# Linear attention into a Swish feed-forward: sharing three pieces of batch 1's preparation differently between engines

## The chip, the cores and the metric

The kernel runs on one core of a Trainium2 chip. A core has a matrix engine (TensorE, "PE" in the profile), a vector engine (VectorE, "DVE"), a scalar engine (ScalarE, "ACT"), a general engine (GpSimd, "POOL") and a sync engine (SyncE, "SP") that here only issues transfers. Each engine runs its own instructions in order and waits on semaphores for others. The metric is device time in microseconds, the median of several executions.

## The reference, cut to what matters

```python
def phi(x):                     # elu(x) + 1
    return np.where(x > 0, x, np.exp(x) - 1.0) + 1.0
q_p, k_p = phi(q), phi(k)                       # 8 batches, 8 heads, 576 rows, 64 columns
kv  = einsum('bhsd,bhse->bhde', k_p, v)
z   = sum(k_p, axis=2)
num = einsum('bhsd,bhde->bhse', q_p, kv)
den = einsum('bhsd,bhd->bhs', q_p, z)[..., None] + 1e-06
x   = (num / den) -> transposed to (4608 rows, 512)
h   = x @ w_in                                  # 512 x 2048
g   = h * (1.0 / (1.0 + np.exp(-beta * h)))     # beta: one number for each of 2048 columns
out = g @ w_out                                 # 2048 x 512
```

## The kernel before, in words

The work goes batch by batch. For each batch the rows are first prepared: phi of q and k (an exp on ScalarE, a max-and-add `r` and a minimum on VectorE), v copied beside a column of ones into `vaug`, the product of k and v (`kv_both`, tile `kvp`), q transposed, the numerators and denominators (`numers`, tile `nps`), their quotient `xs`, and the transpose of that, `xT`. Then come the two matrix products: `h_phase` makes 16 steps of 4 matmuls of 512 columns, each followed by ScalarE's silu into `g`; `y_phase` makes 4 tiles `y_ps` of 16 matmuls each, which are copied to `y_sb` and stored. Each row count is 576 = 4 x 128 + 64; the last 64 rows of all batches are gathered and treated as a ninth round.

The silu is computed with the scale beta, and w_out is divided by beta once: `w_out_scale(i)` multiplies the i-th of four quarters, chunk by chunk (c from 0 to 3), by `rbeta` into bfloat16. The float weights are loaded into space that is free early on (`g`'s second buffer and `stage`).

The order of instructions is written out by hand (`manual_schedule`); the framework adds the semaphore waits that data and buffers need. Batch 0 and 1 are special. While TensorE works on batch 0's y, the other engines prepare batch 1: `phi_all(1, ...)`, `v_copy(..., 1, pr)` for two pairs of heads pr, `q_trans(1, ...)` (transposes on TensorE, four copies to `qT` on ScalarE), `kv_both(1)`, `numers_1`, `numers_1_last`, and `x_trans(1, t, ...)` (transposes on TensorE, a copy to `xT`). Between them, by hand, stand the pieces of batch 0's y: `y_mm(b, t, i, ...)` adds four matmuls (quarter i of w_out) to y tile t. Two more things are put there: the scaling of w_out's last quarter, `w_out_scale(3, (1, 3))`, whose chunks 1 and 3 ScalarE makes and 0 and 2 VectorE, and the exps of batch 2 (`phi_part(2, ...)`), which must come before the first silu of batch 1, as exp and silu need different tables in ScalarE.

PSUM, the memory that TensorE writes to, has eight banks. Four are the ring `mm` (tiles `y_ps`, `h_ps`, one `tp`); a tile gets the slot that was given back longest ago, and waits until its last reader has finished. The other four hold small tiles for batch 0's start and, from batch 1's kv on, two pair tiles of two banks (`num_tile`: `kvp`, `nps`, `tp`, `qop`). In `h_phase` of batch 1, steps 3 and 4 take pair tiles in place of ring tiles. The transposes `qop` (after step 6) and the kv product of batch 2 (after step 8) take pair tiles too.

The loads of q, k, v for the first batches and of the weights are issued from GpSimd's queue at the start; its copies stand in the same queue. Stores and transposing transfers are issued from SP's.

Of the kernel before, what the change touches and what calls it, by code (L numbers as in the profile page):

```python
# [10 lines left out]
ALU = mybir.AluOpType  # L11
# [5 lines left out]
def kernel(  # L17
# [10 lines left out]
    nc = tc.nc  # L28

    B, H, S, D = q.shape  # L30
# [6 lines left out]
    J = S // G  # L37
# [17 lines left out]
    vaug = [consts.tile([P, 2, J, 2, 66], BF16, name=f"vaug{i}") for i in range(2)]  # L55
    w_in_sb = [consts.tile([P, KC, 512], BF16, name=f"w_in{i}") for i in range(4)]
    w_out_sb = [consts.tile([P, 4, DM], BF16, name=f"w_out{i}") for i in range(4)]
# [7 lines left out]
    w_out_f = [  # L65
        a.rearrange("p (c m) -> p c m", c=4)
        for a in (g_f[:, 0:2048], g_f[:, 2048:4096], stage[:, 0:2048], stage[:, 2048:4096])
    ]
# [71 lines left out]
    def phi_part(b, a, pr, x, j0=0, j1=J):  # L140

        if j0 == 0:
            st[b, a, pr, "e"] = work.tile([P, 2, J, D], BF16, tag="e", name="e", bufs=4)
        nc.scalar.activation(st[b, a, pr, "e"][:, :, j0:j1], x[:, :, j0:j1], ACTF.Exp)  # L144
# [17 lines left out]
    def places(b, pr):  # L162

        return slice(2 * pr, 2 * pr + 2) if b == 0 else slice(pr, 4, 2)

    def xin(b, a, pr):
        if b == 0 and a == "q":
            return q0f[:, places(b, pr)]
        return (xk if a == "k" else xq)[b % NX][:, places(b, pr)]

    def v_copy(eng, b, pr):
        src = vb[b % 2] if b < 3 else vf[b % 2]
        eng.tensor_copy(  # L173
            vaug[b % 2][:, pr, :, :, 0:D], src[:, places(b, pr)].rearrange("p h j d -> p j h d")
        )

    def k_quads(b, pr, dst, mov):
# [49 lines left out]
    def num_tile(name):  # L227
        return numps.tile([P, 2, 512], F32, tag="num", name=name)
# [4 lines left out]
    def kv_both(b):  # L233

        t = num_tile("kvp")
        for pr in range(2):
            kv_pair(b, pr, [t[:, hh, pr * EA : (pr + 1) * EA] for hh in range(2)])
        if b == 1:
            nc.vector.tensor_copy(kv1[:, 0], t[:, 0, 0 : 2 * EA])
            nc.scalar.copy(kv1[:, 1], t[:, 1, 0 : 2 * EA])  # L240
            return
        st[b, "kvd"] = work.tile([P, 2, 2 * EA], BF16, tag="kv_bd", name="kvd")
        nc.vector.tensor_copy(st[b, "kvd"], t[:, :, 0 : 2 * EA])

    def copy(eng, dst, src):
        if eng is nc.scalar:
            nc.scalar.copy(dst, src)  # L247
        else:
            eng.tensor_copy(dst, src)  # L249
# [219 lines left out]
    def h_mm(b, x, ff, hp, c0=0, c1=512):  # L469
        for kc in range(KC):  # L470
            nc.tensor.matmul(  # L471
                hp[:, c0:c1],
                w_in_sb[ff // 4][:, kc, (ff % 4) * P : (ff % 4 + 1) * P],
                x[:, kc, c0:c1],
                start=(kc == 0), stop=(kc == KC - 1), skip_group_check=True,
            )

    def silu(b, ff, hp):
        nc.scalar.activation(  # L479
            g_sb[b % 2][:, ff, :], hp, ACTF.Silu, scale=beta_c[:, ff : ff + 1]  # L480
        )

    def mm_tile(name):
        return mmps.tile([P, 512], F32, tag="mm", name=name)

    def y_mm(b, t, i, yp, c0=0, c1=512):
        for c in range(4):
            ff = 4 * i + c
            nc.tensor.matmul(  # L489
                yp[:, c0:c1],  # L490
                g_sb[b % 2][:, ff, t * P : (t + 1) * P],
                w_out_sb[i][:, c, c0:c1],
                start=(ff == 0), stop=(ff == FC - 1), skip_group_check=True,
            )

    def rows(b, j):
        return out[b * S : (b + 1) * S, :].rearrange("(g j) m -> j g m", j=J)[j]

    def y_out(b, t, yp, c0=0, c1=512, queues=(nc.sync, nc.sync), copier=nc.vector):
        y_sb = work.tile([P, DM], F32, tag="y_sb", name="y_sb", bufs=3)  # L500
        copy(copier, y_sb[:, c0:c1], yp[:, c0:c1])
        for i in range(2):
            dst = rows(b, 2 * t + i) if b < B else rows(2 * t + i, J - 1)
            queues[i].dma_start(out=dst[:, c0:c1], in_=y_sb[i * G : (i + 1) * G, c0:c1])
# [28 lines left out]
    def v_copies(b):  # L533
        for pr in range(2):
            v_copy(nc.gpsimd, b, pr)
# [4 lines left out]
    rbeta = consts.tile([P, FC], F32)  # L540
# [183 lines left out]
        if ff == 5:  # L724
            q_odd_trans(0, misc_bf()[:, 0:256])

    def w_out_scale(i, acts=()):
        for c in range(4):
            ff = 4 * i + c
            if c in acts:  # L730
                nc.scalar.mul(w_out_sb[i][:, c, :], w_out_f[i][:, c, :], rbeta[:, ff : ff + 1])
            else:
                nc.vector.tensor_scalar(
                    w_out_sb[i][:, c, :], w_out_f[i][:, c, :], rbeta[:, ff : ff + 1],
                    None, ALU.mult,
                )

    load(nc.gpsimd, xq[2], q, 2)
    load(nc.gpsimd, xk[2], k, 2)
# [2 lines left out]
    for i in range(3):  # L742
        w_out_scale(i)
    yps = [mm_tile("y_ps") for _ in range(4)]
    phi_all(1, "q")
    phi_all(1, "k")
    for i in range(2):
        for t in range(4):
            y_mm(0, t, i, yps[t])
    v_copy(nc.gpsimd, 1, 1)  # L750
    v_copy(nc.vector, 1, 0)
    y_mm(0, 0, 2, yps[0])
    y_mm(0, 1, 2, yps[1])
    q_trans(1, (0, 1), num0_tile().bitcast(BF16), (nc.scalar, nc.scalar))
    y_mm(0, 2, 2, yps[2])
# [1 line left out]
    num0_pool.__exit__(None, None, None)  # L757
    misc_pool.__exit__(None, None, None)
    numps = ctx.enter_context(tc.tile_pool(name="numps", bufs=2, space=bass.MemoryType.PSUM))
    y_mm(0, 3, 2, yps[3], 0, 256)  # L760
    kv_both(1)
    y_mm(0, 3, 2, yps[3], 256, 512)
    w_out_scale(3, (1, 3))
    numers_1()
    phi_tile(2, "q")
# [9 lines left out]
    copies = [x_trans(1, t, nc.scalar, tp[:, t - 1]) for t in (1, 2)]  # L775
    for f in copies:
        f()
    y_out(0, 1, yps[1])
    y_mm(0, 3, 3, yps[3], 0, 256)
    x_trans(1, 3, nc.vector, num_tile("tp")[:, 0].bitcast(BF16))()  # L780
    y_mm(0, 3, 3, yps[3], 256, 512)
    for pr in range(2):
        phi_part(2, "k", pr, xin(2, "k", pr))
    phi_part(2, "q", 1, xin(2, "q", 1))
    y_out(0, 2, yps[2])
    for pr in range(2):
        phi_relu(2, "k", pr, xin(2, "k", pr))
    y_out(0, 3, yps[3])
# [6 lines left out]
    def run(side, n):  # L795
        for f in side.get(n, ()):
            f()

    def h_phase(b, x, side):
        for ff in range(FC):  # L800

            if b == 1 and ff in (3, 4):
                hp = num_tile("h_ps2")[:, 0]
            else:
                hp = mm_tile("h_ps")
            h_mm(b, x, ff, hp)
            silu(b, ff, hp)
            run(side, ff)
# [25 lines left out]
    for b in range(1, B + 1):  # L834
# [22 lines left out]
        if m < B:  # L857
# [7 lines left out]
            if m + 1 < B:  # L865
                at(sy, 10, lambda: phi_exps(m + 1, "k"))
        h_phase(b, xT[b % 3] if b < B else xT_tail, sh)
        y_phase(b, sy, last=(b == B))

# [29 lines left out]
```

## Time and profile before

| | us |
|---|---|
| median of 12 runs | 286.94 |
| lowest, highest | 286.22, 289.76 |
| the profiled execution's own time | 289.11 |
| its span | 287.3 |
| PE busy | 278.0 |
| ACT busy | 162.0 |
| DVE busy | 106.2 |
| POOL busy | 38.0 |

The span runs from the first to the last instruction in the trace; the execution's own time has another 1.8 us around it. In the lines that follow, a chain or timeline line begins with the start in the span and the duration, both in us; L12 is line 12 of the kernel; "out<-in" are tiles; "x8" counts instructions; a bracket gives the idle time of the engine just before, and what ended it. The mean granted clock of TensorE is 0.988 of full speed.

### The profile page before, as it was taken

The numbers are of one execution on the slowest core, as the hardware profiler recorded it, in microseconds if no ns is written. First come the engines' busy times: TensorE is split into PE (matmuls) and PEld (weight loads), VectorE is DVE, ScalarE is ACT, GpSimd is POOL, SyncE is SP. The second block draws the span as 40 slices with busy tenths as digits, with TensorE's granted clock in tenths as the row PEclk, the third lists the DMA queues.
The fourth block names the chain that finished last, engine by engine and source line by source line (L and its number), as shares of the span: only waits on it lengthen the run. The fifth ranks groups of instructions, "written<-read, shape, count | busy, mean of one in ns | idle before, by whom it ended". The sixth has DMA issues, their size and how long they took to land.

```text
span 287.3 us, 5995 instructions
## 1 busy us (share of the span) xinstructions
PE 278.0 (97%) x2504; PEld 140.0 (49%) x2504; DVE 106.2 (37%) x261; ACT 162.0 (56%) x221; POOL 38.0 (13%) x50
## 2 busy tenths in 40 slices
PE   7799998999999999999999999999999999999994
PEld 2585445544664544454445444544444444444443
DVE  5742656912952283128311931191015100110012
ACT  5659866985766861786188707840860076017500
POOL 8622120306002200310040001200000000000000
PEclk9879999999999999999999999999999999999999
DMA  7999999579969946983898349445403410230032
GB/s 217 201 214 390 227 281 194 133 116 265 185 129 264 202 78 147 273 150 78 149 270 147 80 119 263 100 80 137 96 2 79 114 39 0 49 81 19 0 73 74
DMA packets 51723, 41.03 MB, mean 143 GB/s; under 512 B 31584, under 2 KB 43120, under 8 KB 51696
## 3 DMA queue, kind: packets, MB, share of 16 engines
q1 hardware_dynamic: 38800, 23.61, 34.6%
q0 software_dynamic: 12736, 16.91, 30.0%
q8 instruction: 19, 0.31, 0.5%
q10 hardware_dynamic: 160, 0.13, 0.2%
q14 instruction: 8, 0.07, 0.1%
HBM read 36.71 MB, written 9.44 MB: 161 GB/s over the span
## 4 chain that ended last, share of the span: by engine, by line
PE 90%; ACT 5%; DMA 3%; issue 1%; DVE 0%; POOL 0%; DVEq 0%; POOLq 0%
PE y_ps L489 43%; PE h_ps L471 40%; DMA xk<-in_k_dram 3%; ACT e L144 2%; PE h_ps L668 1%; PE nps L315 1%; ACT g L479 1%; PE nps L184 1%; PE kvp L184 1%; ACT xT L247 1%; PE nps L634 1%; PE warm_ps L133 1%; PE nps_m L315 0%; ACT L479 0%; ACT qT L247 0%
## 5 line engine op out<-in xcount | busy, mean ns | idle before, releaser
L479 ACT ACTIVATE g<-h_ps,beta_c 128x512 bf16<-128x512 f32 x144 | 97.7, 689 | 89.0 <-PE h_ps L471 88.5
L489 PE MATMUL y_ps<-w_out,g 128*128 128x512 bf16 (+3 forms) x632 | 127.4, 360 | 0.0
L471 PE MATMUL h_ps<-xT,w_in 128*128 128x512 bf16 x496 | 109.0, 379 | 0.4 <-ACT xT L247 0.3
L489 PEld LDWEIGHTS <-g 128*128 128x128 bf16 x632 | 60.7, 98 | 61.6 <-issue 0.2
L471 PEld LDWEIGHTS <-w_in 128*128 128x128 bf16 x560 | 54.6, 98 | 65.2 <-DVE xT L249 0.4
L249 DVE COPY y_sb<-y_ps 128x512 f32<-128x512 f32 (+2 forms) x36 | 24.2, 672 | 80.3 <-PE y_ps L489 80.3
L421 DVE TENSOR_SCALAR den<-nps 128x12 f32<-128x12 f32 x14 | 2.3, 165 | 63.2 <-PE nps L315 63.2
L144 ACT ACTIVATE e<-xk 128x1152 bf16<-128x1152 bf16 x16 | 17.8, 1156 | 3.6 <-DMA xk<-in_k_dram 2.5
L83 POOL DMA_DIRECT2D xq<-in_q_dram x7 | 5.2, 746 | 93.4 <-DVE phi_k L155 42.7
L144 ACT ACTIVATE e<-xq 128x1152 bf16<-128x1152 bf16 x14 | 15.6, 1156 | 0.1
L412 DVE TENSOR_TENSOR xs<-nps,rden 128x512 bf16<-128x512 f32 (+1 forms) x29 | 15.0, 557 | 0.5
L471 PE MATMUL h_ps<-xT_tail,w_in 128*128 128x512 bf16 x64 | 14.0, 379 | 0.0
L173 POOL CAST vaug<-vf 128x1152 bf16<-128x1152 f32 x10 | 11.2, 1148 | 18.2 <-DMA vf<-in_v_dram 13.9
L155 DVE TENSOR_TENSOR phi_q<-e,r 128x1152 bf16<-128x1152 bf16 (+2 forms) x17 | 11.7, 717 | 2.7 <-ACT e L144 2.4
L155 DVE TENSOR_TENSOR phi_k<-e,r 128x1152 bf16<-128x1152 bf16 x16 | 11.5, 751 | 0.3 <-ACT e L144 0.2
L133 PE MATMUL warm_ps<-xT 128*128 128x512 bf16 x23 | 8.2, 501 | 1.5 <-DVE xT L96 1.5
L144 ACT ACT_TABLE_LOAD x6 | 7.7, 1283 | 2.8 <-DMA xq<-in_q_dram 2.6
L479 ACT ACT_TABLE_LOAD x6 | 7.7, 1283 | 0.1
L148 DVE TENSOR_SCALAR r<-xk 128x1152 bf16<-128x1152 bf16 x16 | 7.6, 509 | 0.4 <-DMA xk<-in_k_dram 0.4
L184 PEld LDWEIGHTS <-phi_k 64*64 64x64 bf16 x576 | 5.9, 108 | 3.6 <-issue 3.6
L83 POOL DMA_DIRECT2D xk<-in_k_dram x9 | 6.8, 755 | 4.7 <-DMA g<-in_moe_w_out_dram 2.0
L173 POOL COPY vaug<-vf 128x1152 bf16<-128x1152 bf16 x3 | 4.0, 1345 | 19.0 <-DMA vf<-in_v_dram 19.0
(96 smaller groups left out, 118.9 us busy)
## 6 DMA issues: line engine op xcount, KB each, us to landing
out_dram<-y_sb SPq DMA_DIRECT2D x70, 128.0 KB, 2.4
vf<-in_v_dram SPq DMA_DIRECT2D x5, 1152.0 KB, 6.6
xq<-in_q_dram POOLq DMA_DIRECT2D x7, 576.0 KB, 9.8
xk<-in_k_dram POOLq DMA_DIRECT2D x7, 576.0 KB, 11.9
w_in<-in_moe_w_in_dram POOLq DMA_DIRECT2D x4, 512.0 KB, 12.9
g<-in_moe_w_out_dram POOLq DMA_DIRECT2D x2, 1024.0 KB, 18.1
stage<-in_moe_w_out_dram POOLq DMA_DIRECT2D x2, 1024.0 KB, 20.6
stage<-in_q_dram SPq DMA_DIRECT2D x2, 576.0 KB, 4.1
```

Source lines behind the costliest of these rows:

```text
L83: return eng.dma_start(out=dst[:, h0 : h0 + n].rearrange("p h j d -> p h (j d)"), in_=rows.rearrange("(i p) e -> p i e", p=P)[:, h0 : h0 + n],
L133: nc.tensor.matmul(warm_ps[:, 0:cols], warm[:, 0:P], warm[:, 0:cols], start=True, stop=True)
L144: nc.scalar.activation(st[b, a, pr, "e"][:, :, j0:j1], x[:, :, j0:j1], ACTF.Exp)
L148: nc.vector.tensor_scalar(r, x, 0.0, 1.0, ALU.max, ALU.add)
L155: nc.vector.tensor_tensor(st[b, a][:, pr, j0:j1].rearrange("p j (h d) -> p j h d", h=2), st[b, a, pr, "e"][:, :, j0:j1].rearrange("p h j d ...
L173: eng.tensor_copy(vaug[b % 2][:, pr, :, :, 0:D], src[:, places(b, pr)].rearrange("p h j d -> p j h d"))
L184: nc.tensor.matmul(dst[hh][c], st[b, "k"][r, pr, j, c], mov(r, j, h), start=(j == 0), stop=(j == J - 1), skip_group_check=True,)
L249: eng.tensor_copy(dst, src)
L412: nc.vector.tensor_mul(out, num, rd[..., None].to_broadcast(list(num.shape)))
L471: nc.tensor.matmul(hp[:, c0:c1], w_in_sb[ff // 4][:, kc, (ff % 4) * P : (ff % 4 + 1) * P], x[:, kc, c0:c1], start=(kc == 0), stop=(kc == K ...
L479: nc.scalar.activation(g_sb[b % 2][:, ff, :], hp, ACTF.Silu, scale=beta_c[:, ff : ff + 1])
L489: nc.tensor.matmul(yp[:, c0:c1], g_sb[b % 2][:, ff, t * P : (t + 1) * P], w_out_sb[i][:, c, c0:c1], start=(ff == 0), stop=(ff == FC - 1), ...
```

## The change

`v_copy` gets a range of the nine groups of rows, and the copy for batch 1's second pair of heads is divided: GpSimd copies groups 0 to 3, ScalarE groups 4 to 8. VectorE copies the first pair as before. In `w_out_scale(3, (1, 3))` chunks 1 and 3 are made by GpSimd instead of ScalarE, and every `y_mm` goes through its four chunks in the order 0, 2, 1, 3. The y piece (tile 3, quarter 2), which stood half before and half after `kv_both(1)`, stands before it whole. The output copy of y tile 1 moves behind the copy of x's fourth tile and behind the exps of batch 2 in the order of the program. In batch 1's `h_phase`, steps 0 and 1 take the pair tiles, where 3 and 4 did.

```diff
-    def v_copy(eng, b, pr):
+    def v_copy(eng, b, pr, j0=0, j1=J):
         src = vb[b % 2] if b < 3 else vf[b % 2]
-        eng.tensor_copy(
-            vaug[b % 2][:, pr, :, :, 0:D], src[:, places(b, pr)].rearrange("p h j d -> p j h d")
+        copy(
+            eng,
+            vaug[b % 2][:, pr, j0:j1, :, 0:D],
+            src[:, places(b, pr), j0:j1].rearrange("p h j d -> p j h d"),
         )
...
     def y_mm(b, t, i, yp, c0=0, c1=512):
-        for c in range(4):
+        for c in (0, 2, 1, 3):
...
-    def w_out_scale(i, acts=()):
+    def w_out_scale(i, pool=()):
         for c in range(4):
             ff = 4 * i + c
-            if c in acts:
-                nc.scalar.mul(w_out_sb[i][:, c, :], w_out_f[i][:, c, :], rbeta[:, ff : ff + 1])
-            else:
-                nc.vector.tensor_scalar(
-                    w_out_sb[i][:, c, :], w_out_f[i][:, c, :], rbeta[:, ff : ff + 1],
-                    None, ALU.mult,
-                )
+            (nc.gpsimd if c in pool else nc.vector).tensor_scalar(
+                w_out_sb[i][:, c, :], w_out_f[i][:, c, :], rbeta[:, ff : ff + 1],
+                None, ALU.mult,
+            )
...
-    v_copy(nc.gpsimd, 1, 1)
+    v_copy(nc.gpsimd, 1, 1, 0, 4)
+    v_copy(nc.scalar, 1, 1, 4, J)
     v_copy(nc.vector, 1, 0)
...
-    y_mm(0, 3, 2, yps[3], 0, 256)
+    y_mm(0, 3, 2, yps[3])
     kv_both(1)
-    y_mm(0, 3, 2, yps[3], 256, 512)
     w_out_scale(3, (1, 3))
...
-    y_out(0, 1, yps[1])
     y_mm(0, 3, 3, yps[3], 0, 256)
     x_trans(1, 3, nc.vector, num_tile("tp")[:, 0].bitcast(BF16))()
     y_mm(0, 3, 3, yps[3], 256, 512)
     for pr in range(2):
         phi_part(2, "k", pr, xin(2, "k", pr))
     phi_part(2, "q", 1, xin(2, "q", 1))
-    y_out(0, 2, yps[2])
+    for t in (1, 2):
+        y_out(0, t, yps[t])
...
-            if b == 1 and ff in (3, 4):
+            if b == 1 and ff < 2:
                 hp = num_tile("h_ps2")[:, 0]
             else:
                 hp = mm_tile("h_ps")
```

## The prediction

> **What bounds the kernel now.** I read the page first: the engines' totals and the chain that ended last.
>
> ```profile
> PE 278.0 (97%) x2504; PEld 140.0 (49%) x2504; DVE 106.2 (37%) x261; ACT 162.0 (56%) x221; POOL 38.0 (13%) x50
> PE 90%; ACT 5%; DMA 3%; issue 1%; DVE 0%; POOL 0%; DVEq 0%; POOLq 0%
> ```
>
> TensorE is the bound, and from 61 us to the end the chain in order of time is TensorE alone. Only what moves TensorE's instructions before that counts. All edits act between 39 and 61 us, so I read the chain there:
>
> ```profile
> 43.11 0.46 PE nps L269 x8
> 43.57 0.02 issue
> 43.59 1.08 ACT qT L247 x2
> 44.67 0.04 issue
> 44.72 0.84 PE kvp L184 x71
> ...
> 45.65 0.30 DVE kv L239
> ...
> 45.98 0.28 ACT kv L240
> ...
> 46.30 0.54 PE nps L315 x44
> 46.84 1.93 PE y_ps L489 x8
> ...
> 49.38 0.58 ACT xT L247
> 49.97 1.06 ACT e L144
> 51.03 0.96 ACT xT L247 x2
> 51.99 3.17 ACT e L144 x3
> 55.16 0.02 issue
> 55.18 1.28 ACT L479
> 56.46 0.01 issue
> 56.47 2.43 ACT g L479 x4
> ```
>
> Two stretches are not TensorE's: batch 1's kv product waits for ScalarE's last qT copy, and from 49.38 to 58.90 ScalarE is full without a gap (exps, x copies, table load, silus). The timeline by engine gives the cover of the moved work and the second stall:
>
> ```profile
> 42.28 1.07 ACT L247 COPY qT<-nps 128x512 bf16<-128x512 bf16 x2 [2.44 <-PE nps L269]
> 39.88 1.76 POOL L173 COPY vaug<-vf 128x1152 bf16<-128x1152 bf16 x1 [9.78 <-DMA vf<-in_v_dram]
> 50.88 2.23 POOL L173 COPY vaug<-vf 128x1152 bf16<-128x1152 bf16 x2 [9.25 <-DMA vf<-in_v_dram]
> 58.94 0.27 PE L288 MATMUL qop<-identity,phi_q 128*128 128x128 bf16 x2 [0.70 <-ACT g L479]
> ```
>
> ScalarE is idle 2.44 us before the qT copies, GpSimd 9.25 us after its v copy, and the qop transposes wait for ScalarE's fourth silu, whose PSUM tile they take.
>
> **What the Trainium skill says.** (1) GPSIMD Engine Reference, "Elementwise — side-by-side cycle accounting": about 1.03 cycles an element for small bodies, 1.8 for an ordinary good loop. The trace agrees for casts: 1148 ns for 1152 float elements. (2) SBUF — State Buffer, "Who interferes with whom": GpSimd and certain VectorE operations lock each other out of a shared port. The trace agrees: GpSimd's v copy took 1756 ns beside VectorE's work at 39.88, and 1137 ns alone. (3) ScalarE: Activation LUTs, "What ACT_TABLE_LOAD costs": 0.833 ns an element; copies lie in every table set by its section on table sets. The trace agrees: no table load stands between exps and copies.
>
> **The change part by part.** Times are those of the profiled execution.
>
> *v in three.* v of batch 1 lands at 39.82 (landing records). GpSimd keeps 4 of 9 groups, 512 elements: 1.14 x 512/1152 = 0.5 us alone, at most about 1.2 with the lockout of 0.62 seen now. ScalarE gets 640: its 512-element copy takes 585 ns, plus 128 x 0.833 = 0.69; the next can start after about 0.65, as copies overlap. It stands behind batch 1's exps, which end at 39.84, and ahead of the qT copies at 42.28: done at 40.6, it is hidden in the 2.44 us. The gain is nothing either: v is ready at 41.63 now, and kvp starts at 44.72 because of qT. Queued behind ScalarE's new wait for v are the four qT copies; the slack is 42.28 - 40.55 = 1.7 us.
>
> *y unsplit ahead of kv.* Half of a y step (4 matmuls of 256 columns, 0.44 us) moves from after kv_both to before it. It fills TensorE's idle time there (43.83 to 44.72), but leaves the wait for the kv copies uncovered (45.5 to 46.0). kvp still starts at 44.72 and numers_1 ends at the same 46.8: zero.
>
> *w_out's last quarter.* Two ScalarE scalings (46.14 to 47.47) become two GpSimd ones. No GpSimd multiply by a column is in the trace. By page (1): 512 x 1.03/1.2 = 0.44 plus some 0.15 of start, to 512 x 1.8/1.2 = 0.77 plus the same: estimates of 0.6 and 0.92 us each. I take 0.8. w_out's quarter lands at 42.47 (landing records), so both end by 43.7 to 44.3, with VectorE idle until 45.65 and no lockout. They are used from 47.2: with the new order 0, 2, 1, 3, VectorE's chunks come first. Cover: 3 us. ScalarE and VectorE already scale parts of this tile at once (46.14 beside 45.86), so the parts do not wait for each other. The gain: now the fourth matmul of y_mm(0,0,3) waits for ScalarE and starts at 47.526 instead of 47.210 + 0.215 = 47.425. So **-0.10**. ScalarE's own 1.33 us only become idle time: its next copy waits for these matmuls, and the chain behind (xT at 49.38) for TensorE. All of it moves 0.10 earlier, the first silu to 56.37. The order 0, 2, 1, 3 elsewhere changes nothing: all chunks are there.
>
> *y's second after x's fourth.* VectorE's y copy (0.68, started at 50.54) now follows x's fourth copy, which starts when its transposes end (51.35 now, 51.25 then). The first h matmul needs that copy, but it also waits for ScalarE's third x copy, which ends at 51.99; so nothing is gained. VectorE idles 0.6 us and its later work shifts by as much at first; but the r of k at 52.29 takes 1139 ns against 445 because GpSimd copies v until 53.11, so most is absorbed. y's two DMAs on SP go about 0.9 later, long before SP's next transposes (58.19). If phi of q came late, the transposes and then GpSimd's q load would, up to the exps at 70.79; ScalarE has 1.80 us idle before the next silu (83.46), which covers it.
>
> *PSUM tiles of h.* Steps 0 and 1, not 3 and 4, take the pair tiles. Those are free as soon as x is, so h starts as ScalarE's x copy ends. Then steps 2 to 5 take the four ordinary tiles, and step 6 needs silu 2. Now TensorE gets through seven steps and then stalls until silu 3 ends (58.89); qop starts at 58.944, step 7 at 59.054. After: it gets through six and stalls until silu 2 ends, 58.31 - 0.10 = 58.21; step 6 from 58.26 (4 x 0.2157 = 0.86), qop 0.11, step 7 at 59.24. So **+0.19** against now, with the 0.10 in it. Everything behind follows TensorE, so the sum is +0.19: 289.11 becomes 289.30.
>
> **From this execution to the median.** The profiled one took 289.11, 2.17 over the median. Its granted clock was 0.68 and 0.63 in the stretches 10 to 15 and 15 to 20 us; I take the difference to lie there, as the rest is TensorE at full clock. Then in the median TensorE comes 2.2 us earlier while loads land as here. qT's first copy would start at 40.08, but after the change only at 40.55, behind ScalarE's v copy: the four copies run back to back, 40.55 + 4 x 0.54 = 42.71 instead of 42.47: +0.24. Together +0.2 to +0.43; I take +0.35: **287.3 us**, no change that a measurement (about 0.5%, 1.43 us) can tell.
>
> **Rivals.** *GpSimd late (slower).* If its scalings end after 47.4, TensorE waits in y_mm(0,0,3), then every ScalarE step behind. It decides from (47.43 - 42.47)/2 = 2.5 us each. GPSIMD Engine Reference, "Instruction dispatch", gives some 6 us for the first call of freshly loaded code: 42.47 + 6 + 1.6 = 50.1, a loss of 2.6: 289.5. Against it: the trace shows GpSimd's configuration instruction at 2.9 us, and its select runs 0.1 us later. 0.09.
>
> *ScalarE's copy holds qT (slower).* If TensorE comes over 3 us earlier against the loads, or v lands as much later, the whole 0.65 shows, and 0.19 with it: 287.8; with v later still, qT follows one for one, up to 1.5: 288.4. For it: v lands only 1.7 us before qT's slack ends. 0.13, of which 0.08 over the bound.
>
> *v bounds kv (faster).* If in the median executions kvp waits for GpSimd's v copy, cutting it from 1.76 to about 0.75 gives 1.0, the unsplit y up to 0.4 and the scaling 0.1: 285.4. For it: v is one of the last loads and ScalarE and GpSimd have idle time. Against: v is ready 3.1 us before kvp here, and still 0.9 before it with TensorE 2.2 us earlier. All TensorE gaps together (0.89 + 0.4 + 0.1 + 0.45 + 0.86) are only 2.7 us. 0.16.
>
> **How the numbers follow.** Forecast 0.62. Its own range is -0.5 to +1.0: 286.4 to 287.9. Adding parts of the rivals until under 0.2 is left out: 285.5 to 288.8. Over 0.5% faster: the v case and little else, 0.15. Slower: GpSimd late 0.09, ScalarE's copy 0.08: 0.17. The rest, 0.68, within.
>
> **What would show it.** Right: the matmuls of y_mm(0,0,3) at even steps; GpSimd's scalings between 42 and 45; an idle TensorE of about 0.5 before and after kvp; a wait of about 1.2 us at h step 6 and none at qop. Wrong: kvp released by something other than qT now or later, GpSimd scalings over 2 us, first silu earlier than 56.2, or TensorE gaps after 62 us.

## The result, and the profile after

| | before | after |
|---|---|---|
| median, us | 286.62 | 287.67 |
| lowest, highest, us | 285.98, 289.89 | 287.33, 288.82 |
| the profiled execution's own time, us | 289.11 | 289.13 |
| its span, us | 287.3 | 287.4 |

The ratio of after to before is 1.0029 with the interval 1.0009 to 1.0048: 0.83 us slower (0.26 to 1.4; the two medians lie 1.05 apart, inside that interval). The change costs a little, less than the 0.5% that one comparison can be relied on to tell, and the forecast of 287.3 us, no change that a measurement can tell, holds. But one term of its sum had the wrong sign, and a wait that matters was not in it.

The page of the kernel after, the engines' totals and the shares of the chain that ended last:

```profile
PE 277.3 (97%) x2500; PEld 138.4 (48%) x2500; DVE 107.4 (37%) x261; ACT 161.4 (56%) x220; POOL 40.9 (14%) x52
PE 90%; ACT 4%; DMA 2%; DVE 1%; issue 1%; POOL 0%; DVEq 0%; POOLq 0%
```

TensorE is still the bound. GpSimd has grown by 2.9 us, where the prediction's two scalings at 0.8 make 1.6, less what the smaller v copy saves, and VectorE has a share of the chain that it did not have. The chain in order of time (start, duration, both in us) says where:

```profile
41.77 1.08 ACT qT L249 x2
42.85 0.04 issue
42.89 0.84 PE kvp L186 x72
...
43.82 0.29 DVE kv L241
44.12 1.62 DVE w_out L732 x2
45.74 0.04 issue
45.78 1.67 PE y_ps L491 x7
...
55.16 1.85 ACT g L481 x3
57.01 0.04 issue
57.05 1.02 PE h_ps L473 x4
...
69.26 12.27 PE y_ps L491 x88
81.53 0.89 issue
82.42 7.93 PE h_ps L473 x36
```

Up to kvp nothing is new: ScalarE's last qT copy releases it. Then VectorE's two scalings of w_out's last quarter stand in the chain for 1.62 us, where before the chain ran over the kv copies straight into TensorE. The wait for a silu has moved from qop to h step 6, at 57.05. And at 81.53 TensorE stops for 0.89 us at the first h step of batch 2, a gap that before does not have. The same place in before's chain:

```profile
70.29 12.27 PE y_ps L489 x88
82.56 7.77 PE h_ps L471 x36
```

The timeline of the kernel after shows the instructions themselves (start, total duration, engine; in brackets the idle time ahead):

```profile
39.48 1.20 POOL L251 COPY vaug<-vf 128x512 bf16<-128x512 bf16 x1 [9.77 <-DMA vf<-in_v_dram]
39.45 0.73 ACT L249 COPY vaug<-vf 128x640 bf16<-128x640 bf16 x1
40.45 1.07 ACT L249 COPY qT<-nps 128x512 bf16<-128x512 bf16 x2 [0.28 <-PE nps L271]
45.78 1.67 PE L491 MATMUL y_ps<-w_out,g 128*128 128x512 bf16 x7 [0.45 <-DVE w_out L732]
57.05 1.02 PE L473 MATMUL h_ps<-xT,w_in 128*128 128x512 bf16 x4 [0.98 <-ACT g L481]
57.91 0.28 PE L290 MATMUL qop<-identity,phi_q 128*128 128x128 bf16 x2
```

The divided copy of v does what the prediction said (GpSimd 1.20 us, ScalarE 0.73). qop follows h step 6 without a wait, as foreseen. The answer for the tile `w_out` between 40 and 48 us gives each duration (least, median, most in ns; then the first and last start):

```profile
L732 POOL TENSOR_SCALAR w_out<-stage,rbeta x2: 1552/1558/1565, 42.3 to 43.9; 128x512 bf16<-128x512 f32 x2
L732 DVE TENSOR_SCALAR w_out<-stage,rbeta x2: 819/887/955, 44.0 to 44.8; 128x512 bf16<-128x512 f32 x2
```

A scaling on GpSimd takes 1.56 us, twice what was estimated. The first ran from 42.32 to 43.89 with VectorE idle, so it is not the shared port that makes it slow. The second, 43.89 to 45.44, then lies over VectorE's two, which take 0.82 and 0.96 us and end at 45.73.

TensorE's granted clock at the front of the program differs from one profiled execution to the next (0.68 and 0.63 of full speed in before's from 10 to 15 and 15 to 20 us, 0.76 and 0.89 in after's, full in e1's), and so does the start of batch 0's y (33.00, 31.18 and 30.41). So absolute starts can't be compared. After's TensorE reaches kvp 1.83 us ahead of before's. I compare stretches between marks that both kernels have:

| stretch, us | before | after |
|---|---|---|
| first y matmul of batch 0 to kvp of batch 1 | 11.72 | 11.71 |
| kvp to the first matmul of y_mm(0,1,3) | 3.02 | 3.53 |
| first silu of batch 1 to qop | 2.47 | 2.75 |
| first y matmul of batch 1 to first h matmul of batch 2 | 14.74 | 15.79 |

So the lead of 1.83 is spent on 0.51 at w_out, 0.28 at the silus, and the last 1.03 at batch 2's h. Everything behind is equal; that is why the two spans agree.

### The profile page after: what moved, and what is told of

It reads as the page before. It is cut to its first block, busy times and chain, and to the rows that moved or that the text cites. A ratio compares the mean times of both kernels' runs of the same rounds, so it can differ in the third digit from the quotient of the medians.

```text
span 287.4 us, 5987 instructions
## 1 busy us (share of the span) xinstructions
PE 277.3 (97%) x2500; PEld 138.4 (48%) x2500; DVE 107.4 (37%) x261; ACT 161.4 (56%) x220; POOL 40.9 (14%) x52
## 4 chain that ended last, share of the span: by engine, by line
PE 90%; ACT 4%; DMA 2%; DVE 1%; issue 1%; POOL 0%; DVEq 0%; POOLq 0%
PE y_ps L491 43%; PE h_ps L473 41%; DMA xk<-in_k_dram 2%; ACT e L144 2%; PE h_ps L670 1%; PE nps L317 1%; PE nps L186 1%; PE kvp L186 1%; ACT g L481 1%; DVE w_out L732 1%; ACT xT L249 1%; PE nps_m L317 0%; PE warm_ps L133 0%; ACT L481 0%; ACT qT L249 0%
## 5 line engine op out<-in xcount | busy, mean ns | idle before, releaser
L732 DVE TENSOR_SCALAR w_out<-g,rbeta 128x512 bf16<-128x512 f32 x8 | 3.8, 536 | 7.3 <-DMA g<-in_moe_w_out_dram 7.3
```

The costliest lines, as they stand in the source:

```text
L732: (nc.gpsimd if c in pool else nc.vector).tensor_scalar(w_out_sb[i][:, c, :], w_out_f[i][:, c, :], rbeta[:, ff : ff + 1], None, ALU.mult,)
```

## The experiments

The runs were made in four groups, each with its own runs of the kernel before on the same chip. The four stretches of the first two groups' profiled executions, in the order of the table above:

| run | to kvp | to y_mm(0,1,3) | to qop | to batch 2's h |
|---|---|---|---|---|
| e1, ScalarE scales again | 11.93 | 3.03 | 2.75 | 14.73 |
| e2, tiles as before | 11.71 | 3.34 | 2.48 | 15.44 |
| e3, both | 12.47 | 3.02 | 2.47 | 14.73 |
| e4, GpSimd's scaling with the chunk order | 11.71 | 4.05 | 2.47 | 14.73 |
| e5, the tiles alone | 11.71 | 3.02 | 2.76 | 14.74 |
| e6, v divided alone | 12.27 | 3.03 | 2.47 | 14.73 |
| e7, y whole and its copy moved, alone | 11.72 | 3.02 | 2.48 | 15.32 |

### The scaling on GpSimd: e1 and e4

e1 is the kernel after with ScalarE's scaling put back; e4 is the kernel before with GpSimd's scaling and the order 0, 2, 1, 3.

```diff
 e1:
-            (nc.gpsimd if c in pool else nc.vector).tensor_scalar(
+            if c in pool:
+                nc.scalar.mul(w_out_sb[i][:, c, :], w_out_f[i][:, c, :], rbeta[:, ff : ff + 1])
+                continue
+            nc.vector.tensor_scalar(
 e4:
-        for c in range(4):
+        for c in (0, 2, 1, 3):
...
-            if c in acts:
-                nc.scalar.mul(w_out_sb[i][:, c, :], w_out_f[i][:, c, :], rbeta[:, ff : ff + 1])
-            else:
-                nc.vector.tensor_scalar(
+            (nc.gpsimd if c in acts else nc.vector).tensor_scalar(
```

> The changed kernel with one part undone: chunks 1 and 3 of w_out's last quarter are made by ScalarE again (in the new order 0, 2, 1, 3). If GpSimd's scaling holds up VectorE's[...], VectorE's two scalings go back from 0.82 and 0.96 us to 0.48 each, the second matmul of y_mm(0,0,3) starts 0.2 us after the first instead of 0.84, and the time falls by 0.5 to 0.6 us against the changed kernel: about 0.3 us over the kernel before. If the loss lies in the PSUM tiles of h or in the landing of batch 2's x instead, the time stays 0.8 us over the kernel before.

> The kernel before with one part of the change: chunks 1 and 3 by GpSimd, and the chunk order 0, 2, 1, 3. If GpSimd's scaling holds up VectorE's, it alone costs 0.5 us or somewhat more, and the trace shows GpSimd's two at about 1.56 us each, VectorE's above 0.8 each. If scaling costs only in company with the rest, the time is that of the kernel before, or 0.1 under it.

Measured: e1 1.0019 (1.0005 to 1.0033), e4 1.0027 (1.0014 to 1.0040). The tile `w_out` in e1:

```profile
L735 DVE TENSOR_SCALAR w_out<-stage,rbeta x2: 476/478/481, 43.5 to 43.9; 128x512 bf16<-128x512 f32 x2
L733 ACT ACTIVATE w_out<-stage,rbeta x2: 708/716/725, 43.8 to 44.4; 128x512 bf16<-128x512 f32 x2
```

With ScalarE beside it, VectorE's scaling of the same 512 elements takes 0.48 us, against 0.82 and 0.96 beside GpSimd, and the stretch is back at 3.03. In e4 the same work alone costs more, 4.05 against 3.02. First the tile `w_out`, then TensorE in its timeline:

```profile
L730 POOL TENSOR_SCALAR w_out<-stage,rbeta x2: 1707/1730/1754, 42.4 to 44.1; 128x512 bf16<-128x512 f32 x2
```

```profile
44.09 0.95 PE L489 MATMUL y_ps<-w_out,g 128*128 128x512 bf16 x3
45.88 1.24 PE L489 MATMUL y_ps<-w_out,g 128*128 128x512 bf16 x5 [0.83 <-POOL w_out L730]
```

Here GpSimd is itself late: TensorE came to this place early, three matmuls went through, and the fourth waited for GpSimd's second chunk, done at 45.83. Two things follow. GpSimd's scaling is the cause of the loss at w_out (e1 has the same chunk order without it, and loses nothing there). And the loss depends on how early TensorE comes, since the load of w_out's quarter, and so GpSimd's start (42.32 to 42.41), does not move with TensorE: 0.31 in e2, where the first of these matmuls starts at 45.22, 0.51 in after (44.94), 1.03 in e4 (44.09). In the timed runs e4 is the only single part whose interval excludes no change. But e1, without GpSimd's scaling, still is 0.54 us over before (0.14 to 0.95), where 0.3 was expected: the timed runs show that the scaling costs time by itself, not that it makes up the whole 0.83.

### The tiles of h: e2, e5, and e3

e2 is after with `ff in (3, 4)` back, e3 is after with this and e1's edit, e5 is before with the tiles of after.

```diff
 e2, and e3 with e1's edit:
-            if b == 1 and ff < 2:
+            if b == 1 and ff in (3, 4):
 e5:
-            if b == 1 and ff in (3, 4):
+            if b == 1 and ff < 2:
```

> The changed kernel with one part undone: in batch 1's h, steps 3 and 4 take the pair tiles again instead of 0 and 1. If the tiles cost what the two traces show (TensorE's lead falls by 0.28 us over step 6 and qop), TensorE again gets through seven steps before it stalls and the time falls by 0.2 to 0.3 us: about 0.5 us over the kernel before. But h step 0 or 1 may now wait for the y tile that VectorE copies later: with y's tile 1 copied at 50.4 to 51.1 that wait is at most 0.4 us at step 1, none if the steps before hide it. If the loss is all in GpSimd's scaling, the time stays 0.8 over.

> The kernel before with one part of the change: batch 1's h steps 0 and 1 take the pair tiles instead of 3 and 4. If the tiles cost what the traces show, from the first silu to the qop transposes it takes 2.75 us instead of 2.47, so 0.28 us over the kernel before. By the prediction's own sum, with nothing else changed, it is the gap of a step of TensorE (0.86) less the spacing of two silus (0.57): 0.29. If the tiles do not matter, no difference from the kernel before.

> The changed kernel with both of these undone; v in three parts, the unsplit y and the moved y copy remain. If scaling and tiles are the whole loss, the time is that of the kernel before within 0.2 us (or 0.1 under it, from the chunk order). If the loss is in what remains, above all in ScalarE's v copy ahead of the qT copies or in the unsplit y, or in the landing of batch 2's x, it stays 0.5 to 0.8 us over.

Measured: e2 1.0030 (1.0014 to 1.0047), e5 1.0010 (0.9991 to 1.0029), e3 1.0025 (1.0003 to 1.0047). TensorE in e5's timeline:

```profile
49.38 5.34 PE L471 MATMUL h_ps<-xT,w_in 128*128 128x512 bf16 x24 [0.29 <-ACT xT L247]
55.70 1.02 PE L471 MATMUL h_ps<-xT,w_in 128*128 128x512 bf16 x4 [0.98 <-ACT g L479]
56.56 0.28 PE L288 MATMUL qop<-identity,phi_q 128*128 128x128 bf16 x2
```

Six steps (24 matmuls), the stall of 0.98 at step 6, none at qop: the prediction's picture, and the stretch to qop is 0.28 longer in every kernel with the new tiles (after, e1, e5) than in those without. As time this is too little to be seen in e5's interval, and e2, with the old tiles, stays 0.86 us over before (0.40 to 1.35), where 0.5 was expected.

e3 has neither of the two costs and still is 0.72 us over before (0.09 to 1.35). By its expectation that points to what remains, and its profile loses 0.75 us before kvp, where ScalarE's copy of v delays the qT copies (next section). But e6 and e7, which hold its parts one by one, show no loss in time, and their intervals overlap with e3's. The timed runs therefore do not settle how the 0.83 us divides; the stretches do that only for the profiled executions.

### The divided v, and the rest: e6 and e7

```diff
 e6:
-    v_copy(nc.gpsimd, 1, 1)
+    v_copy(nc.gpsimd, 1, 1, 0, 4)
+    v_copy(nc.scalar, 1, 1, 4, J)
 e7:
-    y_mm(0, 3, 2, yps[3], 0, 256)
+    y_mm(0, 3, 2, yps[3])
     kv_both(1)
-    y_mm(0, 3, 2, yps[3], 256, 512)
...
-    y_out(0, 1, yps[1])
...
-    y_out(0, 2, yps[2])
+    for t in (1, 2):
+        y_out(0, t, yps[t])
```

> The kernel before with one part of the change: v of batch 1's second pair copied by GpSimd and ScalarE. If ScalarE's copy holds up the four qT copies, the time from the first y matmul to the first kv matmul, 11.72 us where TensorE comes late (first y matmul at 33.0), grows to 11.9 at 30.4 and 12.4 at 30.1, since v lands at 39.4 to 39.8 wherever TensorE is: 0.2 to 0.5 us over the kernel before. If v bounds kv instead, it falls under the kernel before. If ScalarE's copy lies hidden, no difference.

> The kernel before with the remaining parts of the change alone: the y piece unsplit ahead of batch 1's kv, and y's tile 1 copied behind x's fourth tile and the exps. The prediction gave both nothing: from the first kv matmul to the matmuls of y tile 1 the same 3.02 us, h's start and the first silu at the same distance, no difference from the kernel before. If the uncovered wait for the kv copies costs, 0.3 to 0.45 us over it.

Measured: e6 0.9992 (0.9969 to 1.0015), e7 1.0006 (0.9996 to 1.0017). The timeline of e6, ScalarE and TensorE:

```profile
39.45 0.72 ACT L249 COPY vaug<-vf 128x640 bf16<-128x640 bf16 x1
40.08 2.04 ACT L249 COPY qT<-nps 128x512 bf16<-128x512 bf16 x4
42.17 0.80 PE L186 MATMUL kvp<-vaug,phi_k 64*64 64x65 bf16 x72 [1.28 <-ACT qT L249]
```

This is the prediction's rival "ScalarE's copy holds qT": all four qT copies back to back behind the copy of v, and TensorE waits 1.28 us. v lands between 39.4 and 39.8 us in all the runs, wherever TensorE is. The stretch to kvp grows with TensorE's lead: 11.71 where its first y matmul stands at 31.18 (after), 11.93 at 30.41 (e1), 12.27 at 29.90 (e6), and 12.47 at 30.06 (e3, where v landed latest, at 39.8). Up to 0.75 us in a profile, then, yet e6's timed interval goes from 0.9 us faster to 0.4 slower: a small part of this loss may hide in it, and why no more shows in the time was not found out. e7's two local stretches are those of before: both of its edits cost nothing where they are made. Its last stretch is 0.58 longer, and that leads to the wait at batch 2's h.

### What bounds the stretch behind: e9, e10, e11

If a silu wait of 0.70 or 0.98 us is on TensorE's path, more tiles for h should take it away. e9 lets steps 3 and 4, and 6 and 7, share the two banks of a pair tile, and moves qop behind step 9 and the kv product of batch 2 behind step 11; it also gives kv two tiles, one for each copying engine. e10 has no sharing: the pair tiles' pool is closed for the time of four single tiles (steps 3 to 6). e11 is e10 with e9's kv.

```diff
 e9:
-            if b == 1 and ff in (3, 4):
-                hp = num_tile("h_ps2")[:, 0]
+            if b == 1 and ff in (3, 4, 6, 7):
+                if ff in (3, 6):
+                    pair = num_tile("h_ps2")
+                hp = pair[:, 0 if ff in (3, 6) else 1]
...
 e10:
+        if b == 1:
+            numps_pool.__exit__(None, None, None)
+            four_pool = tc.tile_pool(name="fourps", bufs=4, space=bass.MemoryType.PSUM)
+            four = four_pool.__enter__()
...
-            if b == 1 and ff in (3, 4):
-                hp = num_tile("h_ps2")[:, 0]
+            if b == 1 and ff in (3, 4, 5, 6):
+                hp = four.tile([P, 512], F32, tag="four", name="h_ps2")
...
-            at(sh, 6, lambda: q_odd_trans(1, num_tile("qop")[:, 0].bitcast(BF16)[:, 0:256]))
-            at(sh, 8, lambda: kv_both(2))
+            at(sh, 10, lambda: q_odd_trans(1, num_tile("qop")[:, 0].bitcast(BF16)[:, 0:256]))
+            at(sh, 11, lambda: kv_both(2))
 e9 and e11:
+        if b == 1:
+            two = [num_tile("kvp") for _ in range(2)]
...
+            nc.vector.tensor_copy(kv1[0], two[0][:, 0, 0 : 2 * EA])
+            nc.scalar.copy(kv1[1], two[1][:, 0, 0 : 2 * EA])
+            return
```

> A version that may beat both. From the kernel before: batch 1's h takes four tiles from the two pair tiles (both banks of each, steps 3, 4, 6 and 7), the qop transposes move behind step 9 and batch 2's kv behind step 11, so that TensorE need not wait for silus; and batch 1's kv product is written into two tiles and copied to two tiles, so that ScalarE's copy need not follow VectorE's. If TensorE's stall behind ScalarE at qop is what the tiles decide (0.86 us), it goes: 0.8 us under the kernel before, and 0.2 to 0.3 more from the kv copies side by side, 1.0 to 1.1 in all. If ScalarE itself is the bound there and TensorE only waits elsewhere, or if batch 2's x lands too late, little or nothing of this shows.

> A version that may beat both, mended: from the kernel before, batch 1's h takes four single tiles (steps 3 to 6) out of the banks of the two pair tiles, which come back after step 7; qop moves behind step 10, batch 2's kv behind step 11. (Two tiles out of one pair made each step wait for the silu of its neighbour.) If TensorE's stall at qop is a matter of tiles, TensorE goes through steps 0 to 11 without a gap and reaches batch 1's y 0.8 us earlier than in the kernel before. The time falls by 0.8 us, or by less if batch 2's x lands only at 79 us or later, where batch 2's h would begin at 78.9. If ScalarE is the bound, TensorE waits at a later step for the same time and nothing is gained.

> The same, and batch 1's kv product in two tiles, copied by VectorE and ScalarE side by side. From the first kv matmul to the first matmul of y_mm(0,0,3) it took 1.81 us where v was copied in time, against 2.05 in the kernel before, so a further 0.2 to 0.3 us if nothing holds it back; again nothing if batch 2's x lands too late.

Measured: e9 1.0154 (1.0130 to 1.0177), 4.4 us slower where 1.0 to 1.1 faster was expected if the tiles decide; e10 1.0010 (0.9993 to 1.0027), e11 1.0046 (1.0017 to 1.0076). TensorE in e9's timeline:

```profile
49.13 3.61 PE L479 MATMUL h_ps<-xT,w_in 128*128 128x512 bf16 x16 [0.29 <-ACT xT L250]
56.03 4.09 PE L479 MATMUL h_ps<-xT,w_in 128*128 128x512 bf16 x12 [3.29 <-ACT g L487]
```

e9 shares tiles in a way that does harm: step 4 uses the other bank of step 3's tile, but the wait is laid on the whole tile, so it waits for step 3's silu, 3.29 us. In e10, each step with its own tile, the stall is gone:

```profile
49.09 9.66 PE L471 MATMUL h_ps<-xT,w_in 128*128 128x512 bf16 x44 [0.29 <-ACT xT L247]
58.59 0.28 PE L288 MATMUL qop<-identity,phi_q 128*128 128x128 bf16 x2
63.85 1.89 PE L489 MATMUL y_ps<-w_out,g 128*128 128x512 bf16 x8
80.73 1.46 PE L471 MATMUL h_ps<-xT,w_in 128*128 128x512 bf16 x6 [1.98 <-DMA xT<-xs]
```

Eleven steps in a row; from the first h matmul to the first y matmul 14.76 us, against 15.62 in before: 0.86 gained. And the timed median has nothing of it, because TensorE waits 1.98 us at batch 2's h for the transposing transfers of batch 2's x. The last of them landed at 80.64, about when it does in before (80.54), where TensorE comes too late to notice. e11 gains a further 0.26 between kvp and y_mm (1.79 instead of 2.05 to the first matmul of y_mm(0,0,3)) and waits 1.14 at the same place; that its median is worse than e10's is not explained by its profile and stays open.

### What GpSimd's multiply costs: e12

The kernel before, with scratch multiplications and casts added in the last batch's h steps, GpSimd's queue being free there.

```diff
+    def times(eng, dst, n, by):
+        eng.tensor_scalar(dst[:, 0:n], src[:, 0:n], by, None, ALU.mult)
...
+        for n in (256, 512, 1024):
+            times(nc.gpsimd, out16, n, col[0])
...
+        times(nc.gpsimd, out16, 512, 0.5)
+        nc.gpsimd.tensor_copy(out16[:, 0:512], src[:, 0:512])
+        nc.gpsimd.tensor_copy(out16[:, 0:1024], src[:, 0:1024])
```

> The kernel before with scratch operations during batch 7's h, where GpSimd and VectorE are idle: GpSimd multiplies by a column of 256, 512 and 1024 float elements into bfloat16, of 512 into float, of 512 by a constant, casts of 512 and 1024; VectorE's multiply of 512 alone; and both at once. If the multiply itself is slow on GpSimd, it takes about 1.55 us at 512 here too, some 3 ns an element, while casts take 1 ns an element. If the 1.56 us came from VectorE or the loads at that place, it takes 0.6 to 0.9 us here. If the two engines lock each other out, VectorE's multiply takes 0.48 us alone and up to the length of GpSimd's beside it; if not, 0.48 in both places.

The groups of GpSimd in that stretch, shapes kept apart (count, then busy us and mean ns of one, then idle time ahead):

```profile
L839 POOL TENSOR_SCALAR stage<-stage,col 128x256 bf16<-128x256 f32 x1 | 0.9, 925 | 50.1 <-ACT col L836 50.1
L839 POOL TENSOR_SCALAR stage<-stage,col 128x512 bf16<-128x512 f32 x3 | 4.7, 1575 | 0.3
L839 POOL TENSOR_SCALAR stage<-stage,col 128x1024 bf16<-128x1024 f32 x1 | 2.8, 2842 | 0.1
L848 POOL CAST stage<-stage 128x1024 bf16<-128x1024 f32 x1 | 1.1, 1117 | 0.1
```

From 256 to 1024 elements 1.917 us are added, 2.5 ns an element, with about 0.29 us at the start. A cast of 1024 takes 1.117: 1.1 ns an element at most. The rate that the prediction tested on a cast and then used for a multiply does not carry over. This agrees with the 1.56 us of after, and shows that neither a first call nor the loads at that place made it long. The question of the two engines beside each other was not answered as planned: GpSimd was still at work when VectorE's multiplications meant to run alone began, so none of the five ran alone. Beside GpSimd's multiplications and casts they took 0.49, 0.84, 0.49, 0.71 and 1.14 us.

The same run gives a fact on the kernel before itself. Its TensorE came early in this execution (first y matmul of batch 1 at 64.83, against 67.66), and at batch 2's h the timeline has:

```profile
80.62 1.67 PE L471 MATMUL h_ps<-xT,w_in 128*128 128x512 bf16 x7 [0.90 <-issue]
```

The last x of batch 2 landed at 80.53. So the wait is no product of the change: before meets it as soon as TensorE is early enough.

### Moving the loads ahead of batch 2's x: e13

The transfers of batch 2's x are issued while a load of k for batch 4 is under way, and they land only around and after its end: the load at 78.06 and the four x from 78.46 to 80.54 in before, the load at 79.96 and x from 79.96 to 82.32 in after, the load at 78.42 and the second to fourth x from 78.89 to 80.64 in e10. e13 is e10 with the loads of k for batches 3 and 4 issued earlier, into a stretch in which the transfer engines have less to do: in e10 their busy share is 0.41 from 51 to 56 us and 0.23 from 56 to 60, against 1.26 from 70 to 80 (by the trace's count, which can go over 1).

```diff
     load(nc.gpsimd, vb[0], v, 2)
+    load(nc.gpsimd, xk[0], k, 3)
...
     v_copy(nc.gpsimd, 1, 1)
+    load(nc.gpsimd, xk[1], k, 4)
...
-            at(sh, 2, lambda: load_q(3, st[2, "qTd", "dma"]), lambda: load_k(3))
-            at(sh, 2, lambda: load_v(3), lambda: load_k(4))
+            at(sh, 2, lambda: load_q(3, st[2, "qTd", "dma"]))
+            at(sh, 2, lambda: load_v(3))
```

> The version with four single tiles for batch 1's h, in which TensorE reaches the end of batch 1's y at 78.6 us and then waits 2.0 us for batch 2's x, with the loads of k of batches 3 and 4 issued right behind batch 2's v (they were issued after batch 2's q transposes), into the stretch from 51 to 60 us in which the transfer engines stand nearly idle. If batch 2's x lands late because its transposing transfers queue behind these loads, it lands at 77 to 78 us and the wait goes: 1 us or more under the kernel before, about 285.6 us. If it lands late for another reason (the transposes themselves, or v and q of batch 3), the wait stays and the time is that of the kernel before. Batch 0's stores may land later, as they now share the engines with a load.

Measured: 0.9965 (0.9952 to 0.9979), a median of 285.76 us: 1.0 us faster than before (0.6 to 1.4). The two loads of k landed at 55.95 and 59.37 us, instead of 73.89 and 78.42 in e10. The answers for the tile `xT` between 62 and 84 us, time from issue to landing of batch 2's four transposing transfers, first in e10, then in e13:

```profile
DMA to landing us min/median/max: 7.0/9.2/10.2
```

```profile
DMA to landing us min/median/max: 2.5/4.1/5.4
```

And TensorE in e13's timeline:

```profile
63.84 1.89 PE L489 MATMUL y_ps<-w_out,g 128*128 128x512 bf16 x8
66.62 12.12 PE L489 MATMUL y_ps<-w_out,g 128*128 128x512 bf16 x87 [0.16 <-issue]
78.57 7.93 PE L471 MATMUL h_ps<-xT,w_in 128*128 128x512 bf16 x35
```

The same start of batch 1's y as in e10 (63.84, 63.85), and batch 2's h at 78.57 in place of 80.73, without a wait; the last x landed at 75.40, earlier than the 77 to 78 expected. Only the loads differ between the two kernels, so it is the loads that held x up. e10's gain was real and was lost here. The loads moved without e10's tiles, in the kernel before or after, were not run, so how much they bring alone is open.

## Why the prediction was right and where it was wrong

**The time: inside the range, in part by luck.** +0.35 us was forecast and +0.83 (0.26 to 1.4) measured. In the profiled execution the sum was +0.19; by the stretches it was 0.51 + 0.28 = 0.79 up to qop. What kept the forecast near was not its terms: the scaling had the wrong sign, the +0.24 for the median was not confirmed, and the wait behind batch 1, which can swallow gains and losses, was not in the sum.

**w_out's last quarter: the step that failed.** The term "So **-0.10**" measured +0.51 in after, +0.31 in e2 and +1.03 in e4. Three things went into it.

First, "I take 0.8" was 1.56: the estimates of 0.6 and 0.92 came from the lower rates of GPSIMD Engine Reference, "Elementwise — side-by-side cycle accounting". The 1.8 cycles used as the upper bound is there the best case of a tight loop; the same section gives about 2.6 cycles an element for an add of two inputs, which by the clock used there makes an estimate of 1.1 us and was left out of the bounds (the page puts it down to the second input). The measured 2.5 ns an element lies above even that; the measurement decides.

Second, "VectorE idle until 45.65 and no lockout" fell because of the first: scalings of 0.8 would have ended at 43.9, ahead of VectorE's start at 44.03; at 1.56 the second ends at 45.44. SBUF — State Buffer, "Who interferes with whom", names `tensor_scalar` among VectorE's operations that can take the shared port; that agrees with 0.48 us becoming 0.82 and 0.96. It says that the loser blocks for the whole instruction, and this the trace does not show: VectorE's first one began 0.14 after GpSimd's second and ended 0.59 before it.

Third, "Cover: 3 us" was read in the one late execution. The prediction itself has TensorE 2.2 us earlier in the median, but in its sum carries that only into the qT term; with it, the cover of 3 us becomes about 0.8.

The rival "GpSimd late" named the right place, but decided from "2.5 us each". With the prediction's own 2.2 us that limit is (47.43 - 2.2 - 42.47)/2 = 1.4 us, which 1.56 passes, as e4 shows; in after, slower VectorE scalings, which no rival had, were the last to end. The first-call cost that the rival feared did not show: GpSimd's first scaling took 1.565 us, its second 1.552.

**The tiles of h: right.** 0.29 was the term without the 0.10, and 0.28 measured, with the stall at step 6 for silu 2 and none at qop. e5 and e2 give the same.

**v in three: right in kind.** Nothing in the profiled execution (11.71 and 11.72), and "+0.24" for earlier executions: 0.21 to 0.75 in the profiles with TensorE 2.6 to 3.1 us ahead of before's. In time e6 neither confirms nor excludes the +0.24. "v bounds kv (faster)" is refuted where v is copied as in before and TensorE comes early: in e4, e5, e7, e10 and e12 its copy ends 0.3 to 0.7 us ahead of kvp, and qT releases kvp. (Only in e9 was it a copy of v, VectorE's.) One reading of a line was wrong: the GpSimd copy of 1137 ns called "alone" ran beside the r of k whose 1139 ns the prediction names further on. There VectorE gave way, not GpSimd.

**y unsplit, y's second copy: right.** Both zero in e7.

**"Everything behind follows TensorE": wrong.** It holds to the end of batch 1's y. Then batch 2's x decides: its last part landed between 78.6 and 82.3 us in the runs that leave the loads in place, ahead of TensorE by 0.6 to 1.3 us in e1 and e3 to e6, by 1.9 and 2.8 in before and e9, where TensorE came late, and after TensorE had come to this place in after, e2, e7 and e10 to e12. The prediction named TensorE gaps after 62 us as a sign that it is wrong, and there is one of 0.89. So a gain made earlier can be lost there, in part or whole, as e10 and e13 show; that the same wait also evens out the small losses of single parts is only argued, since e5 and e6 have no such wait in their profiles. Why x lands earlier in some executions than in others was not settled.

**Marks.** "First silu earlier than 56.2" was a bad mark: it came at 55.16, only because TensorE's lead at the front was 1.83 us. A mark must be a distance between two instructions.

## What to carry to other kernels

Price an operation on GpSimd by a row of the same operation, not of a cast: here a multiply by a column took 2.5 ns an element where a cast takes 1.1, and it slowed the VectorE work beside it. Where the typical execution differs from the profiled one, carry the shift through every term, above all through the cover of each wait. Follow the bound engine behind the last edit until the next transfer that it waits for: a gain or loss ahead of such a wait says nothing about the time until you know when that transfer lands. If it lands late, look at which loads were issued ahead of it; with single tiles for h in place, moving two of them made the difference between no gain (e10) and 1.0 us (e13).

## What the runs showed of the hardware that was not expected

- GpSimd's multiply of 128 partitions by a column, float to bfloat16: 0.93, 1.58 and 2.84 us for 256, 512 and 1024 elements. By a constant it is no faster (512 elements: 1.65 us, with VectorE at work beside it).
- VectorE's multiply of 512 elements, 0.48 us beside ScalarE, took 0.82 and 0.96 us beside GpSimd's in after and 0.62 and 0.96 in e2, but in e4 one of its two stayed at 0.48 and the other took 0.82. GpSimd's own took 1.56 us with VectorE idle and 1.71 to 1.75 in e4. Which of the two engines gives way is not the same each time.
- Transposing transfers issued behind large loads took 7.0 to 10.2 us to land, and 2.5 to 5.4 us with two of the loads moved away (e10 and e13).
